# First weight block converted as two halves, with a new hand-written order on every engine

## The chip, the core and the metric

The kernel runs on one core of one Trainium2 chip. The core has a matrix engine (PE, with its weight loads shown as PEld), three elementwise engines (DVE, ACT, POOL) and a queue engine, SP, which issues all DMA transfers of this kernel. The metric is the device time of one execution in microseconds (us), from the chip's own clock; lower is better.

## The reference

The computation has two parts. The first is a linear attention with a decaying state, over 4 batches, 8 heads, 768 tokens and 48 values per head:

```python
def _attn_ref(r, k, v, w, u):
    state = np.zeros((B, H, D, D), dtype=np.float32)
    for t in range(S):
        kt, vt, rt = (k[:, :, t], v[:, :, t], r[:, :, t])
        cur = np.einsum('bhd,bhe->bhde', u[None] * kt, vt)
        y[:, :, t] = np.einsum('bhd,bhde->bhe', rt, state + cur)
        state = w[None, :, :, None] * state + np.einsum('bhd,bhe->bhde', kt, vt)
```

Its output, reshaped to 3072 tokens by 384 columns, goes through a feed-forward net (FFN) with 2048 inner columns:

```python
    h = x @ w_in
    sp = np.maximum(h, 0.0) + np.log1p(np.exp(-np.abs(h)))
    g = h * erf(sp)
    return (g @ w_out).astype(np.float32)
```

## The kernel before

**Attention.** The 768 tokens of each batch are cut into chunks of 128, which gives 24 chunks (6 per batch), numbered so that chunk g belongs to batch g mod 4. Each chunk is loaded by SP, its r and k are scaled (`prep_r`, `prep_k`), the matrix of token pairs is made on PE (`a_step`, tiles A), masked into `am` by DVE, and multiplied with the values on PE (`y_step`, tile y). `ds_product` makes what the chunk adds to the state `sbd`. Four chunks make one FFN input block of 512 tokens: ACT writes the high part of x from y (`x_hi`), DVE the low part (`x_lo`).

**FFN.** There are 6 blocks of 512 tokens and 16 slices of 128 inner columns, which gives 96 steps, numbered 0 to 95. Step n is `f1` (9 matmuls of 512 columns into a tile h, of which there are three), six ACT and two DVE operations on it (`act_a` to `act_h`; the last, `act_h`, casts to `gh`), a subtraction to `gl` (`act_l`, DVE or POOL), and `f2` (9 matmuls into three accumulators). The tiles s1, s2, gh and gl have two buffers each. Two matrices of the split-precision weights stand in SBUF, a high part and a low one (`wih`, `wil` for the input side, `woh`, `wol` for the output side).

**Weights.** The weights arrive as 64-bit floats in 8 blocks of 768 columns per matrix. `fetch_w` loads a block, `load_w` converts it in six parts: a (ACT), b, c and d (DVE), e (ACT, the high part) and f (DVE or POOL, the low part). The working tile wt has one buffer, so that one block is in conversion at a time. A block of the input side serves two FFN slices; the first block serves slices 0 and 1. The names C00a to C00f in the order stand for the six parts of the first input block.

**Order.** No scheduler decides the order. `ORDER` is a list of some 1,750 words that is read from left to right, and each word issues one operation; each engine works through its own operations in that order and waits where an operand is not there. A letter names the operation (f, a, b, z, c, d, e, g, h, l and p are those of an FFN step, in this order; A, P, Y, X, D, S, M, Q, N, K, R, E belong to attention; L and F are loads, C the conversions, O the output). The number is the chunk, the step or the block. A trailing + puts the operation on POOL, a * on ACT, neither on DVE; @ names PSUM banks. W with a number is that many dummy matmuls on a tile of zeros (`keep_warm`), of which there are 16 before the first word and 10 in the list. `late.close()` frees the staging tiles after the last C word.

**The end.** The last step is 95. Its three outputs are copied out of the accumulators by ACT (o95_0 and o95_2, the latter in two halves) and DVE (o95_1) and sent by SP. The word Z (`count_bad`) makes a count on PE and DVE that every engine reads with a TENSOR_LOAD, since a general path behind a branch handles decays outside a range.

Of the kernel before, what the change touches and what calls it, by code (L numbers as in the profile page):

```python
# [848 lines left out]
N3* C10a W2 L4b Q4a+ Q4b V2@h L5a W3 M20* L3b C10b Q4c T0 D3@2 C10c P20 Y2@h M40+ M41* C10d L5b Q5a C10e C10f+ K5+ N4
F01 R5+ Q5b Q5c X1b A4@h3 N2* S3a* S3b* Y3@0 X2a D2@h X3a X2b S2b* X3b f0 C01a P41 S2a C01b P40 L6a C01c R6 M51* L6b  # L850
Q6a+ M50* a0 K6 C01d b0 F02 z0 Y4@1 X4a A5@43 P51 C01e C01f+ f1 D4@0 c0 P50 d0 Q6b+ X4b S4b S4a e0 g0 L7a C02a C02b
Q6c C02c a1 b1 Y5@4 X5a X5b z1 f2 M60* c1 C02d C02e K7 M61+ A6@41 d1 N5 f3 P61 D5@2 P60 C02f+ S5b h0 a2 N6+ e1 S5a g1
F11 L7b C11a b2 C11b h1 l0 Y6@0 z2 a3 b3 D6@2 X6a S6b S6a c2 d2 l1+ e2 f4 C11c p0 p1 a4 Q7a C11d z3 C11e g2 h2 C11f
Q7b+ Q7c f5 l2+ c3 X6b F03 C03a C03b C03c p2 C03d R7 d3 e3 g3 M71* A7@01 C03e C03f f6 F12 a5 h3 l3+ b4 P71 b5 C12a z4
c4 z5 a6 C12b C12c M70+ P70 c5 d4 e4 C12d d5 g4 p3 C12e C12f e5 g5 L9a h4 l4+ Y7@1 X7a F13 X7b f7 b6 z6 h5 f8 a7 C13a
l5 C13b C13c b7 c6 d6 L9b Q9a+ e6 z7 c7 d7 C13d F05 C13e e7 K9 p4 g6 h6 p5 f9 a8 F14 g7 h7 l6 C13f+ p6 l7+ p7 b8 z8
L8a K8+ C05a C05b C05c a9 b9 z9 c8 d8 e8 C05d g8 c9 O70a O70b h8 f10 R9 f11 R8 C05e C05f d9 e9 g9 Q9b Q9c l8+ a10 O72a
O72b M91+ b10 z10 C14a h9 l9 O71a a11 b11 A9@01 S4c f12 p8 p9 c10 d10 z11 c11 e10 S4d+ C14b C14c d11 e11 g10 h10 C14d
M90 C14e l10 L8b C14f+ g11 a12 b12 z12 f13 a13 P90 h11 l11+ c12 Q8a+ Q8b+ F04 b13 z13 d12 e12 p10 g12 C04a C04b C04c
N9 c13 d13 f14 p11 f15 a14 C04d b14 h12 S5d l12 C04e C04f p12 F15 e13 g13 Q8c M80+ a15 b15 f16 z14 h13 l13+ P91 z15  # L860
c14 A8@01 d14 e14 p13 C15a c15 g14 d15 e15 C15b a16 h14 C15c f17 b16 C15d C15e S5c+ g15 O71b N7 l14 h15 f18 a17 M81+
b17 z16 c16 d16 e16 l15+ z17 P81 c17 C15f+ P80 p14 p15 F06 C06a O150a g16 h16 d17 a18 O152a C06b C06c e17 f19 C06d b18
a19 Y9@0 O150b l16 g17 h17 l17+ N8 O151a C06e z18 C06f b19 z19 D7@1 F07 p16 c18 C07a C07b F16 C07c d18 e18 c19 d19 g18
# [130 lines left out]
```

## Time and profile before

| | |
|---|---|
| time, median of 3 runs | 507.01 us (506.83 to 507.46) |
| profiled execution, own time | 506.34 us |
| its span, first to last instruction | 504.6 us |
| PE busy | 489.5 us, 97% of the span |
| PEld busy | 384.1 us, 76% |
| ACT busy | 401.4 us, 80% |
| DVE busy | 356.1 us, 71% |
| POOL busy | 200.8 us, 40% |
| chain that ended last, by engine | PE 93%, DVE 3%, ACT 2%, issue 1% |
| chain, by line | L540 (f1) 41%, L599 (f2) 40%, all attention products under 3% each |

The shares of busy time are averages over the whole span, while the limits differ by stage. A stage is therefore read by its own window. "Granted clock" (PEclk) is the share of TensorE's full clock that the chip gave it: 1.00 is 2.4 GHz, 0.50 is 1.2 GHz. An idle time is shown with what ended it.

### The profile page before, as it was taken

The numbers are of one execution on the slowest core, as the hardware profiler recorded it, in microseconds if no ns is written. First come the engines' busy times: TensorE is split into PE (matmuls) and PEld (weight loads), VectorE is DVE, ScalarE is ACT, GpSimd is POOL, SyncE is SP. The second block draws the span as 40 slices with busy tenths as digits, with TensorE's granted clock in tenths as the row PEclk, the third lists the DMA queues.
The fourth block names the chain that finished last, engine by engine and source line by source line (L and its number), as shares of the span: only waits on it lengthen the run. The fifth ranks groups of instructions, "written<-read, shape, count | busy, mean of one in ns | idle before, by whom it ended". The sixth has DMA issues, their size and how long they took to land.

```text
span 504.6 us, 11104 instructions
## 1 busy us (share of the span) xinstructions
PE 489.5 (97%) x4463; PEld 384.1 (76%) x4464; DVE 356.1 (71%) x574; ACT 401.4 (80%) x772; POOL 200.8 (40%) x185
## 2 busy tenths in 40 slices
PE   7799999999999999999999999999999999999993
PEld 3567877777877788777777887778777787878882
DVE  7999999989887777776888758475465675424531
ACT  4778999999988878868678687768886977888881
POOL 6656434352352665236867644103212521121010
PEclk9989999999999999999999999999999999999998
DMA  8647453522741423214522340500120010100001
GB/s 310 215 166 268 147 176 126 182 99 57 257 162 31 148 96 136 83 50 183 158 96 65 123 150 2 188 1 21 31 108 22 6 38 1 62 1 0 1 1 68
DMA packets 15737, 50.92 MB, mean 101 GB/s; under 512 B 1856, under 2 KB 2752, under 8 KB 15680
## 3 DMA queue, kind: packets, MB, share of 16 engines
q1 hardware_dynamic: 15680, 50.15, 29.2%
q8 instruction: 37, 0.61, 0.5%
q14 instruction: 20, 0.16, 0.1%
HBM read 43.85 MB, written 6.29 MB: 99 GB/s over the span
## 4 chain that ended last, share of the span: by engine, by line
PE 93%; DVE 3%; ACT 2%; issue 1%; POOL 0%; DMA 0%; DVEq 0%; ACTq 0%
PE h L540 41%; PE acc L599 40%; PE y L474 3%; PE y L326 2%; PE A L300 2%; PE A L442 2%; PE ds L493 1%; PE kt L389 0%; DVE att L350 0%; DVE am L448 0%; PE dummy L104 0%; POOL att L363 0%; DMA wu<-in_wcol_dram 0%; DVE att L354 0%; DVE pw L193 0%
## 5 line engine op out<-in xcount | busy, mean ns | idle before, releaser
L540 PE MATMUL h<-x,wih 128*128 128x512 f32 x576 | 184.0, 400 | 0.4 <-ACT sbd L505 0.4
L583 POOL TENSOR_TENSOR gl<-s,gh 128x512 fp32r<-128x512 f32 x46 | 61.9, 1346 | 178.6 <-ACT gh L578 159.6
L540 PEld LDWEIGHTS h<-x,wih 128*128 128x128 f32 x576 | 106.7, 188 | 27.8 <-ACT x L514 0.7
L599 PE MATMUL acc<-gh,woh 128*128 128x512 f32 x288 | 115.8, 402 | 0.0
L599 PE MATMUL acc<-gl,woh 128*128 128x512 f32 x288 | 114.5, 398 | 0.2 <-DVE gl L583 0.2
L599 PE MATMUL acc<-gh,wol 128*128 128x512 f32 x288 | 114.1, 396 | 0.0
L540 PE MATMUL h<-x,wil 128*128 128x512 f32 x288 | 114.1, 396 | 0.0
L572 DVE SCALAR_TENSOR_TENSOR s<-s,h 128x512 f32<-128x512 f32 x96 | 65.4, 684 | 60.2 <-ACT s L568 59.7
L556 DVE SCALAR_TENSOR_TENSOR s<-s,h 128x512 f32<-128x512 f32 x96 | 65.5, 684 | 37.9 <-ACT s L551 21.7
L560 ACT ACTIVATE s<-s 128x512 f32<-128x512 f32 x96 | 60.1, 627 | 21.2 <-DVE s L556 20.9
L547 ACT ACTIVATE s<-h 128x512 f32<-128x512 f32 x96 | 56.4, 589 | 24.9 <-PE h L540 24.6
L578 ACT CAST gh<-s 128x512 fp32r<-128x512 f32 x96 | 58.6, 614 | 20.8 <-PE acc L599 9.5
L599 PEld LDWEIGHTS acc<-gh,woh 128*128 128x128 f32 x288 | 54.2, 188 | 14.1 <-issue 0.4
L599 PEld LDWEIGHTS acc<-gl,woh 128*128 128x128 f32 x288 | 54.3, 188 | 13.6 <-DVE gl L583 1.1
L540 PEld LDWEIGHTS h<-x,wil 128*128 128x128 f32 x288 | 54.2, 188 | 13.1
L599 PEld LDWEIGHTS acc<-gh,wol 128*128 128x128 f32 x288 | 54.2, 188 | 13.0
L564 ACT ACTIVATE s<-s 128x512 f32<-128x512 f32 x96 | 60.0, 628 | 1.8
L568 ACT ACTIVATE s<-s 128x512 f32<-128x512 f32 x96 | 60.1, 628 | 1.5
L551 ACT ACTIVATE s<-s 128x512 f32<-128x512 f32 x96 | 60.2, 629 | 1.1
L583 DVE TENSOR_TENSOR gl<-s,gh 128x512 fp32r<-128x512 f32 x50 | 37.3, 748 | 14.1 <-ACT gh L578 13.6
L279 POOL TENSOR_TENSOR am<-att,wr 64x512 f32<-64x512 f32 (+1 forms) x13 | 18.1, 1389 | 7.8 <-PE y L326 7.3
L408 POOL TENSOR_TENSOR att<-att 128x384 f32<-128x384 f32 x12 | 14.5, 1209 | 14.7 <-DVE att L404 12.7
(164 smaller groups left out, 572.6 us busy)
## 6 DMA issues: line engine op xcount, KB each, us to landing
att<-in_late_att_dram SPq DMA_DIRECT2D x12, 640.0 KB, 5.2
att<-in_att_dram SPq DMA_DIRECT2D x12, 512.0 KB, 4.9
raw<-in_win_dram SPq DMA_DIRECT2D x8, 768.0 KB, 6.3
raw<-in_wout_dram SPq DMA_DIRECT2D x8, 768.0 KB, 5.3
att<-in_late_att_dram SPq DMA_DIRECT2D x12, 512.0 KB, 4.0
att<-in_att_dram SPq DMA_DIRECT2D x8, 608.0 KB, 5.5
out_dram<-o SPq DMA_DIRECT2D x17, 256.0 KB, 2.8
att<-in_late_att_dram SPq DMA_DIRECT2D x12, 256.0 KB, 2.9
```

The source lines that it names most:

```text
L279: eng.tensor_tensor(out=late_am(g, half)[r], in0=by_head(chunks[g][r, 0:512]), in1=wr[r].rearrange("p a (b c) -> p (a b) c", b=2), op=ALU. ...
L540: nc.tensor.matmul(out=h, lhsT=w[:, f, q, :], rhs=x[:, xi, q, :], start=k == 0, stop=k == 8)
L547: nc.scalar.activation(out=s1, in_=e["h"], func=AF.Tanh, bias=FB0, scale=FA0)
L551: nc.scalar.activation(out=s1, in_=s1, func=AF.Tanh, bias=FB1, scale=FA1)
L556: nc.vector.scalar_tensor_tensor(out=e["s"], in0=e["s1"], scalar=FG, in1=e["h"], op0=ALU.mult, op1=ALU.add)
L560: nc.scalar.activation(out=s, in_=s, func=AF.Tanh, bias=FB2, scale=FA2)
L564: nc.scalar.activation(out=s, in_=s, func=AF.Square, bias=FB3, scale=FA3)
L568: nc.scalar.activation(out=s, in_=s, func=AF.Square, bias=FB4, scale=FA4)
L572: nc.vector.scalar_tensor_tensor(out=s, in0=s, scalar=FC, in1=ff[n]["h"], op0=ALU.subtract, op1=ALU.mult, reverse0=True)
L578: nc.scalar.copy(out=e["gh"], in_=e["s"])
L583: eng.tensor_tensor(out=e["gl"], in0=e["s"], in1=e["gh"].bitcast(F32), op=ALU.subtract)
L599: nc.tensor.matmul(out=acc[e], lhsT=w[:, f, es], rhs=g, start=first and i == 0, stop=last and i == 2)
```

## The change

The first 768 input columns are no longer converted in one pass of six parts. `load_w` makes two passes of 384 columns, C00a to C00f for the columns of slice 0 and C08a to C08f for those of slice 1; both read the same loaded block and both use the one working tile.

```diff
     def load_w(part, eng, which, g):
-        words = raws[which, g].bitcast(I32).rearrange("p (n two) -> p n two", two=2)
+        first = which == 0 and g in (0, NG)
+        c0, n = (g // NG * WG // 2, WG // 2) if first else (g * WG, WG)
+        raw, o = (raws[0, 0], c0) if first else (raws[which, g], 0)
+        words = raw[:, o:o + n].bitcast(I32).rearrange("p (n two) -> p n two", two=2)
         wl, wh = words[:, :, 0], words[:, :, 1]
         if part == "a":
-            bits[which, g] = stage.tile([P, WG], I32, tag="wt", name=f"wt{which}{g}", bufs=WTB)
+            bits[which, g] = stage.tile([P, WG], I32, tag="wt", name=f"wt{which}{g}", bufs=WTB)[:, 0:n]
...
-        s = slice(g * WG, (g + 1) * WG)
+        s = slice(c0, c0 + n)
...
-WG, RAWB, WTB = 768, 2, 1
+WG, NG, RAWB, WTB = 768, 8, 2, 1
...
 ORDER = """
-L0a K0 V0@0 L3a K3 W2 L1a R0 E0 K1 W3 R3 B0@1 J0* E3+ H0 Q0c* R1 A0@2h M00* P00 B3@1 J3* F00 H3 V1@h E1 L2a L0b L2b
+L0a K0 L3a L1a W2@2 L0b R0 E0 F00 B0@3 R3 J0* H0 K1 L2a C00a R1 E1 V0@h A0@10 V1@4 K3 C00b U0 Q0c* M00* P00 B1@h N0*
...
-b95 z95 h94 c95 d95 l94+ p93y p94z e95 p94x p94y g95 h95 l95 p95y O951a p95z O952a p95x O950a O951b O952b Z0 O950b
+l95 p95y p95z p95x O952a O950a O950b O951a O952b Z0 O951b
 """
```

The whole list is written anew: 1,762 words in place of 1,755. The operations are the same but for the six added parts and two dummy matmuls more (12 in the list in place of 10); their order, their PSUM banks and the choice between DVE, POOL and ACT differ on every engine. Line numbers after the diff's first hunk are 3 higher.

**Place 1, DVE ahead of FFN step 0.** wt00 and wt08 are the working tiles of the two conversions, raw00 the loaded block, am*c*_*h* the masked pairs of chunk c, x0 the input of block 0, which `f1` of step 0 reads. Before, a stretch with the conversion of all 768 columns:

```order
L137 TENSOR_SCALAR wt00_280<-wt00_280 128x768
L425 TENSOR_TENSOR am1_0_328<-ident_97,q1_320 128x512
L139 SCALAR_TENSOR_TENSOR wt00_280<-raw00_246,wt00_280 128x768
L354 TENSOR_TENSOR att2_255<-att2_255,wre_118 112x512
L448 COPY_PREDICATED am1_1_322<-mask_98,A1_1_303 128x512
L448 COPY_PREDICATED am1_0_328<-mask_98,A1_0_302 128x512
L142 SCALAR_TENSOR_TENSOR wt00_280<-raw00_246,wt00_280 128x768
L448 COPY_PREDICATED am3_1_386<-mask_98,A3_1_346 128x512
L375 COPY att2_255<-qp2_398 128x128
```

After, a stretch that ends at the low part of chunk 1 in x0:

```order
L520 TENSOR_TENSOR x0_356<-y0_281,x0_356 128x3x128
L378 COPY att2_205<-qp2_366 128x128
L140 TENSOR_SCALAR wt08_379<-wt08_379 128x384
L508 COPY sbd_160<-ds1_347 48x4x48
L142 SCALAR_TENSOR_TENSOR wt08_379<-raw00_194,wt08_379 128x384
L145 SCALAR_TENSOR_TENSOR wt08_379<-raw00_194,wt08_379 128x384
L357 TENSOR_TENSOR att4_321<-att4_321,wr_116 112x512
L353 TENSOR_TENSOR att4_321<-att4_321,wk_117 112x512
L520 TENSOR_TENSOR x0_356<-y1_392,x0_356 128x3x128
```

The three DVE parts of the second half (wt08) stand behind the low part of chunk 0 and ahead of that of chunk 1, so that they are ahead of step 0, whose `f1` reads all four chunks of x0.

ACT at the same place, up to its first operation of step 0 (s1_0 from h0). Before:

```order
L423 ACTIVATE am4_1_527<-ident_97,q4_475 128x128 x4
L145 CAST woh_91<-wt10_449 128x768
L396 COPY att2_255<-kt2_457 128x4x48 x2
L505 COPY sbd_160<-ds3_497 48x4x48 x2
L514 CAST x0_405<-y2_508 128x3x128
L514 CAST x0_405<-y3_568 128x3x128
L505 COPY sbd_160<-ds2_586 48x4x48
L135 ACTIVATE wt01_609<-raw01_539 128x768
L423 ACTIVATE am5_1_619<-ident_97,q5_543 128x128 x4
L423 ACTIVATE am5_0_626<-ident_97,q5_543 128x128 x4
L547 ACTIVATE s1_0_631<-h0_599 128x512
```

After:

```order
L426 ACTIVATE am2_0_529<-ident_97,q2_430 128x128 x4
L508 COPY sbd_160<-ds2_518 48x4x48
L426 ACTIVATE am4_0_575<-ident_97,q4_527 128x128 x4
L517 CAST x0_356<-y3_534 128x3x128
L148 CAST woh_91<-wt10_483 128x768
L517 CAST x0_356<-y2_553 128x3x128
L426 ACTIVATE am4_1_586<-ident_97,q4_527 128x128 x4
L138 ACTIVATE wt01_616<-raw01_509 128x768
L426 ACTIVATE am5_0_618<-ident_97,q5_614 128x128 x4
L550 ACTIVATE s1_0_637<-h0_625 128x512
```

Here 10 groups of four `am` activations stand ahead of step 0 in place of 8 on the whole engine; the added ones are for chunks 0, 1 and 4 (one each) while one of chunk 5 moved behind.

**Place 2, PE between steps 2 and 3.** A6 is the pair matrix of chunk 6, h3 the tile of step 3. Before:

```order
L442 MATMUL A6_0_785<-att6_615 64x128
L442 MATMUL A6_1_786<-att6_615 64x128
L540 MATMUL h3_805<-x0_405,wih_89 128x512 x2
L540 MATMUL h3_805<-x0_405,wil_90 128x512
L540 MATMUL h3_805<-x0_405,wih_89 128x512 x2
```

After:

```order
L445 MATMUL A6_0_776<-att6_580 64x128
L445 MATMUL A6_1_777<-att6_580 64x128
L104 LDWEIGHTS warm_86
L104 MATMUL dummy_804<-warm_86 128x512
...
L104 MATMUL dummy_804<-warm_86 128x512
L543 MATMUL h3_808<-x0_356,wih_89 128x512 x2
L543 MATMUL h3_808<-x0_356,wil_90 128x512
```

Three dummy matmuls now stand between A6 and step 3. The operand of A6 is scaled by `prep_r` of chunk 6, on DVE before and on POOL after. The tile of step 1 (h1) follows that of step 0 directly now.

**Place 3, the end on SP.** o95_1, o95_20, o95_21 and o95_0 are the outputs of step 95, fi the count. Before:

```order
L611 DMA out_dram<-o95_1_5614 128x512
L609 DMA out_dram<-o95_20_5619 128x256
L609 DMA out_dram<-o95_21_5620 128x256
L649 TENSOR_LOAD fi_180
L649 ISA x2
L611 DMA out_dram<-o95_0_5626 128x512
```

After:

```order
L614 DMA out_dram<-o95_0_5612 128x512
L612 DMA out_dram<-o95_20_5608 128x256
L612 DMA out_dram<-o95_21_5609 128x256
L652 TENSOR_LOAD fi_180
L652 ISA x2
L614 DMA out_dram<-o95_1_5615 128x512
```

The output that is sent first is o95_0 in place of o95_1, and o95_1 is the one behind the TENSOR_LOAD. On ACT and DVE the copies of the outputs stand as before.

## Rows read from the trace of the kernel before

**Rows 1.** Page, busy time and share of the span by engine, with instructions.

```profile
PE 489.5 (97%) x4463; PEld 384.1 (76%) x4464; DVE 356.1 (71%) x574; ACT 401.4 (80%) x772; POOL 200.8 (40%) x185
```

**Rows 2.** Windows: stretch in us, its length, busy time of each engine (x instructions), granted clock, DMA share, GB/s.

```profile
34.60:490.00 455.40, 455.36 (x3974) 361.69 (x3975) 323.74 (x504) 375.89 (x700) 178.54 (x154) 1.00 0.28 93
37.90:106.20 68.30, 68.30 (x618) 53.91 (x607) 63.82 (x97) 64.84 (x116) 31.35 (x23) 1.00 0.49 172
7.20:35.00 27.80, 22.88 (x449) 15.95 (x447) 25.23 (x41) 19.14 (x61) 17.02 (x14) 0.88 0.62 225
10.75:37.90 27.15, 23.09 (x469) 17.18 (x474) 24.64 (x40) 20.39 (x62) 16.50 (x11) 0.87 0.60 207
```

**Rows 3.** Windows of 2 us each in the start, the same columns.

```profile
20.00:22.00 2.00, 1.07 (x40) 0.80 (x31) 2.00 (x2) 0.60 (x2) 0.78 (x1) 1.00 0.90 342
24.00:26.00 2.00, 2.00 (x34) 1.67 (x34) 0.90 (x2) 2.00 (x7) 1.76 (x2) 0.50 0.98 301
```

**Rows 4.** Chain of waits in order of time: start, us, what.

```profile
24.05 1.92 PE A L442 x32
27.68 1.28 PE dummy L104 x3
34.64 2.51 PE h L540 x9
```

**Rows 5.** Timeline, ACT: start, us, instruction; then DVE.

```profile
10.77 0.27 ACT L375 COPY att<-qp 128x128 f32<-128x128 f32 x1 [1.92 <-DVE att L350]
16.18 1.28 ACT L423 ACTIVATE am<-ident,q 128x128 f32<-128x128 f32 x4
37.93 0.60 ACT L547 ACTIVATE s<-h 128x512 f32<-128x512 f32 x1
33.31 1.65 DVE L517 TENSOR_TENSOR x<-y,x 128x384 fp32r<-128x384 f32 x3
```

**Rows 6.** Groups of ACT, then POOL, by form: count, busy us, mean ns, idle before.

```profile
L145 ACT CAST wih<-wt 128x768 fp32r<-128x768 f32 x8 | 6.7, 837 | 3.1 <-DVE wt L142 3.1
L514 ACT CAST x<-y 128x384 fp32r<-128x384 f32 x24 | 11.1, 472 | 3.9 <-PE y L474 3.4 <-PE y L326 0.5
L354 POOL TENSOR_TENSOR att<-att,wr 112x512 f32<-112x512 f32 x2 | 3.1, 1548 | 0.0
```

**Rows 7.** Timeline, DVE and POOL side by side near 20 us.

```profile
19.50 2.10 DVE L142 SCALAR_TENSOR_TENSOR wt<-raw,wt 128x768 int32<-128x768 int32 x1
19.73 1.04 POOL L425 TENSOR_TENSOR am<-ident,q 128x512 f32<-128x512 f32 x1
```

**Rows 8.** Timeline, PE: dummy matmuls.

```profile
2.37 5.29 PE L104 MATMUL dummy<-warm 128*128 128x512 bf16 x16 [2.37 <-ACT warm L98]
27.48 1.49 PE L104 MATMUL dummy<-warm 128*128 128x512 bf16 x3
```

**Rows 9.** Timeline near 107 us: PE, then DVE, around step 12.

```profile
107.70 0.50 PE L599 MATMUL acc<-gl,woh 128*128 128x512 f32 x1
106.96 0.69 DVE L583 TENSOR_TENSOR gl<-s,gh 128x512 fp32r<-128x512 f32 x1
```

**Rows 10.** Timeline of the end: SP, ACT, DVE; then SP's longest own wait.

```profile
496.27 0.33 SPq L611 DMA_DIRECT2D out_dram<-o  x1
496.70 0.88 SPq L609 DMA_DIRECT2D out_dram<-o  x2
496.95 0.58 ACT L630 COPY o<-acc 128x512 f32<-128x512 f32 x1
497.08 0.15 DVE L648 TENSOR_REDUCE fi<-cnt 1x1 int32<-1x4 f32 x1 [0.76 <-PE cnt L647]
498.67 0.34 SPq L611 DMA_DIRECT2D out_dram<-o  x1
SPq L747 <- SPq L747: 2.7, 1, 2.7
```

More of the change, by code (lines that the diff above doesn't have):

```diff
@@ L849 @@
[L849 to L863, printed above, removed]
@@ new lines @@
+d10 l9 e10 z11 C14b g10 c11 C14c p8 d11 C14d F15 a12 p9 e11 g11 R8+ f13 h10 l10 C14e b12 a13 M91+ h11 C14f+ z12 f14
+l11 c12 b13 C04a z13 c13 C04b p10 d12 C04c e12 g12 N7+ O72b p11 f15 S5d+ d13 e13 K8+ C04d F06 h12 P91 g13 l12+ C04e
+C04f+ a14 O71b a15 P90 b14 h13 z14 l13+ b15 p12 C15a z15 C15b c14 d14 e14 f16 A8@01 c15 p13 d15 g14 e15 C15c h14 l14+
+C15d C15e g15 h15 f17 p14 a16 C15f l15 M81+ b16 a17 z16 b17 S6c+ N9+ C06a c16 z17 d16 P81 e16 p15 g16 c17 O150a F07
+f18 M80+ C06b C06c h16 P80 d17 l16+ e17 a18 g17 b18 C06d f19 h17 D7@3 D9@1 z18 O151a O150b O152a S7a a19 C06e l17+
@@ new lines @@
+Y9@0 S7b L10a p16 C06f c18 d18 L11a F16 S9a b19 z19 C07a C07b L11b O151b c19 C07c e18 d19 f20 g18 C07d e19 h18 C07e
+g19 p17 a20 C07f h19 l18 l19 b20 z20 O231a C16a C16b c20 f21 a21 S9b C16c f22 d20 p18 b21 F17 C16d z21 e20 p19 a22
+L10b g20 C16e c21 D8@1 Q10a+ C16f h20 S6d d21 b22 C17a K11 e21 l20 z22 c22 C17b f23 Q10b+ g21 d22 C17c e22 C17d a23
+p20 g22 h21 C17e b23 l21+ f24 h22 C17f f25 z23 S7d c23 l22 S7c+ d23 e23 g23 a24 a25 b24 p21 Q11a h23 O152b z24 l23
+O230a b25 c24 Q11b z25 Q11c d24 e24 X9a p22 R10+ c25 p23 S4c O231b X9b f26 d25 g24 Q10c h24 O231c e25 a26 g25 Y8@0 b26
@@ new lines @@
+R12a+ p30 S11b h31 l31 L14b L12c z32 S11a b33 R13a z33 O311a c32 d32 e32 c33 p31 d33 f34 e33 O311b S8c+ O312a a34
+O311c g32 h32 f35 g33 A12@01 h33 f36 b34 l32+ z34 M121* Q14a+ c34 d34 S9c+ a35 O310a O312b L13c e34 O310b l33+ G12a
+b35 a36 P120 p32 p33 g34 Q14b+ f37 Q14c z35 K14+ P121 h34 G12b+ S12a N13+ c35 b36 l34 d35 e35 g35 S10c+ z36 h35 c36
+d36 A13@01 G13a G13b+ a37 b37 l35+ S13a p34 f38 e36 P131 a38 P130 g36 O312c z37 c37 d37 Y13@0 h36 X13a Y12@1 M141 e37
+l36+ L15a L15b g37 M140 b38 f39 a39 b39 z38 p35 p36 c38 R14a f40 h37 R14b+ L16a d38 K15+ L16b e38 l37 S11c+ g38 z39
@@ new lines @@
+l51 c52 L22a a53 N19+ b53 d52 z53 e52 X17a g52 p50 f54 L22b p51 f55 R21b+ L19c a54 X17b c53 h52 A19@01 b54 d53 Q19c
+l52 z54 M191 M190+ e53 g53 p52 c54 d54 h53 l53 a55 R21a e54 b55 f56 Q21a z55 c55 d55 P190 L21c g54 a56 e55 b56 P191
+Q21b+ h54 f57 p53 l54 g55 z56 h55 c56 Q21c d56 e56 G19a a57 f58 p54 b57 l55+ G19b+ a58 z57 g56 p55 h56 f59 Y19@0 b58
+c57 d57 e57 g57 l56 h57 z58 O472b Q22a f60 a59 c58 d58 K21 p56 e58 b59 l57 S19a z59 L20a X19a c59 a60 S18c+ d59 g58
+e59 p57 b60 X19b g59 h58 h59 f61 l58 N21 z60 f62 M210+ a61 b61 l59+ c60 z61 d60 e60 a62 A21@10 R20a p58 c61 g60 Q22b+
@@ L911 @@
+g91 c92 p89 a93 d92 e92 h91 g92 O792b p90 l91 b93 z93 f94 h92 c93 d93 a94 l92 b94 e93 z94 g93 c94 p91 h93 O791b l93
+f95 d94 e94 a95 b95 g94 z95 p92 h94 c95 d95 p93y e95 l94+ p93x p93z p94y p94x g95 h95 p94z l95 p95y p95z p95x O952a
+O950a O950b O951a O952b Z0 O951b
 """
```

90 lines of the change are left out of this document (42 added, 48 removed).

## The prediction, made before the change was run

> **What bounds the kernel now.** I read the page's busy time first, then windows by stage, then the chain of waits. PE is busy for 489.5 us [rows 1], but that is an average of three stages. From the first FFN step to 490 us PE is busy 455.36 of 455.40 us at the full clock [rows 2]. There is nothing to win inside that stage except work taken off PE; every other engine has idle time there, but not everywhere: from 37.9 to 106.2 us ACT is busy 64.84 of 68.30 us and DVE 63.82 [rows 2], so that stage is nearly bound by three engines at once. Ahead of it lies the start, where PE waits for attention chunks to become x, and behind it the end. So the change can act in three ways: by the time at which step 0 can run, by new waits or new work on PE in the full stage, and by the end.
>
> The chain of waits through the start shows what sets step 0. PE idles near 21 us, its clock falls to 0.50 in the 2 us from 24.00 [rows 3], and the chain then runs through PE at half speed: the A products take 1.92 us and three dummies in that chain 1.28 us; step 0 starts at 34.64 [rows 4]. It starts before x is complete: DVE writes the low parts of the last three chunks in 1.65 us from 33.31 [rows 5], to 34.96, and the second matmul of step 0 reads them. That 34.96 is the number to compare.
>
> **The split itself.** The promise is that slice 1's half is converted behind the work for step 0. On DVE the order says otherwise: the three parts of the half wt08 stand ahead of the low part of chunk 1, and its two ACT parts ahead of the high parts of chunks 1 and 3. All six parts are still ahead of step 0. The split defers nothing past step 0, and it adds an instruction per part. A cast of 384 columns takes 472 ns against 837 ns for 768 [rows 6], so two cost 0.11 us more. No row shows the other parts at half size; I take the same 0.1 us for each of them, between 0 (exactly half) and 0.4 (a half costs three quarters of the whole). This is small, and it is counted inside the walk below.
>
> **When step 0 can run (-1.5 us).** What does change is the start's order. I walked the three engines by hand through the new order with durations of before, at the full PE clock. ACT takes the copy of the first q at 10.77 [rows 5] about 0.5 us earlier, since one scaling of another chunk is moved behind the product that it waits for. From there ACT has more to do until its first operation of step 0: ten groups of four `am` activations at 1.28 us [rows 5] instead of eight, 2.56 us, and 0.2 us for the halves, with small copies nearly in balance, so about 2.6 us more. Before, ACT is busy 20.39 of 27.15 us in that stretch [rows 2]. So it has 23.0 us of work from 10.3, and cannot reach step 0 before 33.3; with all of the old idle time it would reach it at 40.0. In the walk it has few waits, because the `am` groups no longer wait for POOL and PE: X high parts of chunks 0 and 1 near 19.0 and 22.8, the decay table `wkn` near 27.5, chunk 2's at 32.4, step 0's first activation near 36 instead of 37.93 [rows 5]. DVE waits once, near 27, for POOL's products on chunk 4, and finishes the last low part near 33.4. That is 1.5 us ahead of 34.96. Bounds: DVE is busy 25.23 of the 27.80 us from 7.20 [rows 2] and by count has the same work ahead of step 0 as before, so that it cannot finish before 32.4, 2.6 us ahead; on the other side 1.0 us behind, if PE's clock falls as before and ACT waits as before.
>
> What could help further is contention. The last DVE part of the first conversion took 2.10 us while a POOL operation of 1.04 us ran beside it [rows 7]; POOL has about 4 us less to do ahead of step 0 now. I count nothing for it, since the walk already uses the short duration; it is why the walk may hold. The Trainium skill, GPSIMD Engine Reference, section 1, Specifications, says that POOL's SBUF interfaces are shared with VectorE and contended by DVE instructions with two SBUF inputs; the stretched row has two such inputs, so the trace agrees there. By that rule alone the gain would be 1.1 us larger if before's sum had been walked with the short form; by the rows it stays at 1.5.
>
> **Dummies on PE (+0.6 us).** Three dummy matmuls now stand between A6 and step 3, in the full stage. Before, no dummy is there. Sixteen cost 5.29 us in a row, 0.33 each with the slow beginning; three at the half clock 1.49 us [rows 8]. At the full clock I take 0.2 us each, so 0.6 us, if PE has work waiting. The lower bound is 0, if PE waits at that place anyway; the upper is 1.5.
>
> **ACT and POOL behind step 0 (+0.9 us).** The walk gives more reasons to wait there. `prep_r` of chunk 6 moves from DVE to POOL, where the operation takes 1.55 us [rows 6], behind a conversion part that itself waits for ACT; A6 would wait for it up to 0.7 us, and the dummies and step 3 are queued behind A6 on PE. Then, up to the cast of step 12, ACT has about 2.3 us more (three groups of `am` come in, one goes out, some small operations move), while it had 3.46 us idle in the 68.30 us of this stretch [rows 2]. How near the edge that is can be seen at step 12: its `gl` is written in 0.69 us from 106.96, to 107.65, and PE takes it at 107.70 [rows 9]. There is no slack, and that `gl` goes to POOL in the new order. So of the start's gain, what the dummies leave is lost at the latest there: ACT begins its FFN work some 1.9 us earlier, has 2.3 us more to do, and POOL takes longer for the last link. I take 0.9 us, which makes PE even with before at step 12; bounds 0 (ACT uses its idle time) and 2.4 (it does not, and step 14 waits as well). Once lost, it stays lost, since PE is full from there to 490.
>
> **The rest of the full stage (0).** The FFN work and the attention groups are the same, the number of times that attention cuts into FFN work is the same within one. New orders of DVE, POOL and ACT are hidden as long as `gl` leads `f2`. Before, PE waits nowhere in this stage, so a new order can only equal that or lose: 0, with up to 1 us of loss.
>
> **The end (+1.3 us).** Here the order decides alone. Before, SP sends o95_1 at 496.27 and two halves from 496.70, for 0.88 us, then reads the count (ready at 497.23), and issues the last output at 498.67, 1.09 us after the halves; its data were ready at 497.53 [rows 10]. Now SP's first item is o95_0, the output that is ready last. The halves, ready long before, are queued behind it, and the TENSOR_LOAD and o95_1 behind them: issue of o95_0 near 497.6, halves to 498.9, the count's 1.09 us, last issue near 500.0. That is 1.3 us later, and the program ends after the last transfer (SP's wait of 2.7 us [rows 10]). ACT, DVE and PE finish at the same places, so nothing hides it. Bounds 0.9 and 1.7. In PE's last steps one `f2` fewer stands behind `f1` of step 95, which may give or cost half a microsecond; I count 0.
>
> **Sum.** -1.5 + 0.6 + 0.9 + 0 + 1.3 = +1.3 us. Against the profiled execution's 506.34 us this is 507.6; that execution was 0.7 us under the median of the three runs, 507.01, whose own range is 0.6 us. Against the median: **508.3 us**, 0.26% slower.
>
> **Rivals.**
> 1. *The start's gain is kept.* ACT uses its idle time, so the 0.9 falls away, or the dummies lie in a wait: -1.5 + 0.6 + 1.3 = +0.4, about 507.4, within 0.2%. For it speaks that DVE has some 2 us less to do up to step 12; against it the missing slack at step 12. Chance 0.30.
> 2. *Faster: the start runs without waits.* Before, the chain ran through PE at half speed; its two rows of 1.92 and 1.28 us [rows 4] would take half that at full speed, 1.6 us less, and DVE waited meanwhile (busy 0.90 of the 2 us from 24.00 [rows 3]). The new order spreads its dummies (1, 3 and 3 from about 23 to 27 us in the walk). If that keeps the clock up and DVE then works without a wait, the last low part is ready near its bound, 32.4; with the later dummies in a wait and no loss behind them this gives -2.6 + 1.3 = -1.3, so 505.7. It decides from a last low part before 32.7. Chance 0.14.
> 3. *The clock falls elsewhere, or ACT's debt is full.* In the walk PE idles 1.9 us near 8 to 10 us, because of the five dummies that stood there two are left, right behind the first sixteen; before, 0.93 us of idle time in the 2 us from 20.00 came ahead of the fall [rows 3]. A fall there would double the first A products and set the start back by up to 2 us: 510. The Trainium skill, TensorE: Matmul & The Clock Gate, section "What's actually happening", has the clock follow how busy PE has been lately, with the low level as the default; the trace agrees, as its fall follows an idle PE. By that rule the new gap is a danger and the price is that of this rival. Chance 0.14, with the full debt at step 14 (509.8) in it.
> 4. *The change does not do what it says.* That holds for the split in any case, as shown; if the reordered start gives nothing either, the sum is +0.6 to +1.3 plus 0.2, near 508.3, and no different from the forecast.
>
> **Chances and range.** The forecast, with rival 4, has 0.42. What can be told from no change here is about 0.2%, 1.0 us. The forecast's own spread, 507.4 to 509.4, puts a good part of it within that; with rivals 1 and 3: slower 0.48, same 0.37, faster 0.15. The range leaves out most of rival 2 and the worst of rival 3: 506.3 to 510.0.
>
> **What would show it.** The last output issue on SP about 1.4 us behind ACT's copy of o95_0 plus the halves' time, and a longer stretch from PE's last matmul to the end, by 1.3 us. DVE's last low part before step 0 near 33.4 and ACT's first activation of step 0 near 36. Three dummies ahead of step 3 without idle time before them. Waits of PE on `gl` or on A6 between 38 and 115 us, where before has none. The prediction is wrong if SP issues the last output no later, if the low part is ready before 32.7 and PE stays full, or if PE waits after 120 us.

## The result, and the profile after

The changed kernel takes 512.55 us (median of four executions, 511.33 to 513.64), the kernel before 507.24 beside it (506.83 to 507.93): a ratio of 1.011, interval 1.009 to 1.0129. It is slower, as forecast, but by 5.3 us where 1.3 were forecast, and outside the range of 506.3 to 510.0. The profiled execution took 511.33 us with a span of 509.3, against 506.34 and 504.6 before.

PE has as much to do as in [rows 1] and spends more of the span on nothing. From the page of the changed kernel, the busy times and then the chain that ended last:

```profile
PE 488.6 (96%) x4466; PEld 382.7 (75%) x4466; DVE 372.8 (73%) x582; ACT 397.7 (78%) x754; POOL 192.5 (38%) x179
...
PE 76%; DVE 13%; ACT 6%; issue 2%; DMA 1%; POOL 1%; SPq 0%; DVEq 0%; ACTq 0%; POOLq 0%
```

The share of PE in the chain fell from 93% to 76%, and DVE has 16.7 us more busy time though its instructions are nearly the same ones. Both point at DVE. The timeline of PE names the places; these are the idle times from step 0 on that it marks, and the three dummies (start, us, instruction, and in brackets the idle time before it and what ended it). The line at 47.27 is D5, the product that chunk 5 adds to the state:

```profile
31.60 0.49 PE L543 MATMUL h<-x,wih 128*128 128x512 f32 x1 [1.38 <-ACT x L517]
...
32.65 0.50 PE L543 MATMUL h<-x,wih 128*128 128x512 f32 x1 [0.56 <-DVE x L520]
...
43.73 0.82 PE L104 MATMUL dummy<-warm 128*128 128x512 bf16 x3
...
47.27 0.56 PE L496 MATMUL ds<-att 128*48 128x48 f32 x16 [0.62 <-DVE am L451]
...
79.30 0.73 PE L543 MATMUL h<-x,wih 128*128 128x512 f32 x2 [0.76 <-DVE s L575]
...
106.05 0.73 PE L543 MATMUL h<-x,wih 128*128 128x512 f32 x2 [0.17 <-DVE s L575]
...
275.75 0.33 PE L303 MATMUL A<-am,att 48*64 48x64 f32 x3 [0.68 <-DVE x L520]
...
284.57 0.50 PE L602 MATMUL acc<-gl,woh 128*128 128x512 f32 x1 [3.01 <-DVE gl L586]
...
499.12 0.51 PE L602 MATMUL acc<-gl,woh 128*128 128x512 f32 x1 [0.20 <-DVE gl L586]
```

In windows (stretch, length, busy time of PE, PEld, DVE, ACT and POOL, granted clock, DMA share, GB/s) the stage that answers to [rows 2] is full from 115 us on but for one piece:

```profile
37.00:47.00 10.00, 9.55 (x157) 6.90 (x153) 9.62 (x16) 9.38 (x23) 9.51 (x8) 1.00 0.59 203
47.00:57.00 10.00, 9.53 (x165) 7.92 (x166) 9.11 (x16) 9.91 (x20) 6.28 (x6) 1.00 0.55 187
115.00:255.00 140.00, 140.00 (x1376) 111.19 (x1378) 118.26 (x184) 110.87 (x202) 68.31 (x62) 1.00 0.36 121
255.00:290.00 35.00, 31.15 (x392) 24.15 (x380) 30.62 (x38) 21.57 (x38) 20.03 (x19) 1.00 0.30 99
290.00:490.00 200.00, 200.00 (x1498) 160.20 (x1497) 115.72 (x179) 156.35 (x281) 41.35 (x35) 1.00 0.12 42
```

Two of these stretches in the kernel before:

```profile
37.00:47.00 10.00, 10.00 (x195) 7.88 (x198) 9.79 (x16) 8.76 (x19) 6.54 (x5) 1.00 0.69 256
255.00:290.00 35.00, 35.00 (x563) 27.66 (x562) 29.36 (x41) 26.81 (x54) 25.31 (x22) 1.00 0.31 102
```

From 255 to 290 us PE is idle for 3.85 us; before, it was busy 35.00 of the same 35 us. In that stretch the biggest wait is 3.01 us, for `gl` of step 47. DVE, and below it POOL, at that place:

```profile
273.16 1.35 DVE L345 TENSOR_TENSOR att<-sbd,w 48x384 f32<-48x384 f32 x1
...
275.73 0.69 DVE L292 TENSOR_TENSOR am<-ident,q 64x512 f32<-64x512 f32 x1
...
278.41 4.91 DVE L292 TENSOR_TENSOR am<-ident,q 64x512 f32<-64x512 f32 x1
...
283.84 0.68 DVE L586 TENSOR_TENSOR gl<-s,gh 128x512 fp32r<-128x512 f32 x1
...
272.81 1.29 POOL L282 TENSOR_TENSOR am<-att,wr 48x512 f32<-48x512 f32 x1 [5.00 <-PE y L329]
...
277.52 1.29 POOL L282 TENSOR_TENSOR am<-att,wr 64x512 f32<-64x512 f32 x1
278.77 0.82 POOL L339 TENSOR_TENSOR att<-att,w 48x384 f32<-48x384 f32 x1
279.56 1.29 POOL L353 TENSOR_TENSOR att<-att,wk 112x512 f32<-112x512 f32 x1
280.82 1.00 POOL L361 TENSOR_TENSOR att<-att,wkn 128x384 f32<-128x384 f32 x1
281.78 0.98 POOL L407 TENSOR_TENSOR att<-att,ub 128x384 f32<-128x384 f32 x1
```

The same DVE instruction takes 0.69 us at 275.73. The next one begins at 278.41 and is held until POOL's five operations, which follow each other without a gap, have ended at 282.76; what is left after that is the 0.6 us of its own work. Behind it on DVE stands, after one operation of 0.67 us, the `gl` that step 47 needs. The wait of 0.68 us at 275.75, for a low part of x from DVE, looks the same: the DVE product at 273.16 takes 1.35 us where it takes 0.55 later (at 347.96), and ends 0.41 us behind POOL's operation of 272.81. A long DVE instruction is not a loss of PE's by itself: at 265.49 a `gl` took 2.87 us beside POOL and PE did not wait, and before, the longest stretched ones of this stretch took 1.77 to 1.86 us, with PE full.

The start, on the other hand, went better than forecast. The last low part of x0, on DVE, which answers to [rows 5], and two windows of the start, to [rows 3]:

```profile
32.05 0.55 DVE L520 TENSOR_TENSOR x<-y,x 128x384 fp32r<-128x384 f32 x1
```

```profile
24.00:26.00 2.00, 2.00 (x52) 1.48 (x51) 2.00 (x3) 1.36 (x4) 1.59 (x2) 1.00 0.78 260
34.00:36.00 2.00, 2.00 (x10) 1.62 (x9) 1.95 (x4) 1.97 (x7) 0.05 (x1) 1.00 0.78 318
```

It is ready at 32.60, 2.36 us ahead of the 34.96 before, and the clock stays at 1.00. The end on SP, which answers to [rows 10]:

```profile
501.92 0.33 SPq L614 DMA_DIRECT2D out_dram<-o  x1
502.30 0.93 SPq L612 DMA_DIRECT2D out_dram<-o  x2
504.26 0.33 SPq L614 DMA_DIRECT2D out_dram<-o  x1
```

The whole difference of the two profiled executions, 4.99 us, adds up like this. The first matmul of the last `f2` that reads `gl` comes at 499.12 in place of 494.78, 4.34 us later. Behind D5 at 47.27, PE waits for 0.20 (to 57 us) + 0.93 (at 79 and 106) + 3.85 (255 to 290) = 4.98 us; so at 47.3 it must still have been 0.64 us ahead (4.98 less 4.34). Of the 2.36 us of lead at step 0, 1.72 are gone by then. From 499.12 to the end of the span it takes 10.18 us against 9.82, 0.36 more; the time outside the span is 2.03 against 1.74, 0.29 more. 4.34 + 0.36 + 0.29 = 4.99.

### The profile page after: what moved, and what is told of

The parts are those of the page before. It is cut to its first block, busy times and chain, and to the rows that moved or that the text cites. A ratio compares the mean times of both kernels' runs of the same rounds, so it can differ in the third digit from the quotient of the medians.

```text
span 509.3 us, 11107 instructions
## 1 busy us (share of the span) xinstructions
PE 488.6 (96%) x4466; PEld 382.7 (75%) x4466; DVE 372.8 (73%) x582; ACT 397.7 (78%) x754; POOL 192.5 (38%) x179
## 4 chain that ended last, share of the span: by engine, by line
PE 76%; DVE 13%; ACT 6%; issue 2%; DMA 1%; POOL 1%; SPq 0%; DVEq 0%; ACTq 0%; POOLq 0%
PE h L543 35%; PE acc L602 34%; PE y L329 2%; PE y L477 2%; PE A L303 1%; DVE wt L142 1%; DVE wt L145 1%; DVE s L575 1%; DVE am L292 1%; DVE s L559 1%; ACT am L426 1%; DVE gl L586 1%; DMA att<-in_att_dram 1%; DVE wt L140 1%; ACT wt L138 1%
## 5 line engine op out<-in xcount | busy, mean ns | idle before, releaser
L586 POOL TENSOR_TENSOR gl<-s,gh 128x512 fp32r<-128x512 f32 x41 | 56.1, 1371 | 193.9 <-ACT gh L581 182.5
L586 DVE TENSOR_TENSOR gl<-s,gh 128x512 fp32r<-128x512 f32 x55 | 44.5, 812 | 19.9 <-ACT gh L581 19.7
L282 POOL TENSOR_TENSOR am<-att,wr 64x512 f32<-64x512 f32 (+1 forms) x12 | 15.9, 1327 | 22.7 <-PE y L329 22.5
L407 POOL TENSOR_TENSOR att<-att,ub 128x384 f32<-128x384 f32 x11 | 12.0, 1092 | 23.3 <-DMA att<-in_att_dram 21.1
```

Source lines behind the costliest of these rows:

```text
L282: eng.tensor_tensor(out=late_am(g, half)[r], in0=by_head(chunks[g][r, 0:512]), in1=wr[r].rearrange("p a (b c) -> p (a b) c", b=2), op=ALU. ...
L586: eng.tensor_tensor(out=e["gl"], in0=e["s"], in1=e["gh"].bitcast(F32), op=ALU.subtract)
```

## The experiments

A border is the moment at which one POOL operation ends and the next, right behind it, begins. **Theory.** DVE instructions whose operands lie in SBUF stand still while POOL works, for whole rows of POOL operations; the new order puts such a row beside the DVE work that feeds step 47. **Rival.** DVE and ACT are simply late since the start, and the waits would come without POOL. Times of before differ by a few tenths from one comparison to the next, so each kernel is set against the median of before that ran beside it. An order is changed by moving words; a word's letter, number and mark are those of the section on the kernel before.

**The split alone.** The order of before, with the second half's parts put in behind the first's.

```diff
-C00f+ Q2c M21* P30 V3@2 X0b
+C00f+ C08a Q2c C08b M21* C08c P30 C08d V3@2 C08e X0b C08f+
```

> The order of the kernel before, with only the split put in: the six parts of the first half stand where the six parts of the whole block stood, the six parts of the second half one by one behind them, all ahead of step 0. If the split itself costs about 0.1 us per part and hides beside other work, as predicted, the time is 507.0 to 507.8 us. If the split is what costs, because the second half sits on DVE and POOL in front of step 0, it is 509 us or more and step 0 starts later than 35.5 us.

510.89 us against 507.66 (ratio 1.0058, interval 1.0036 to 1.008). The parts' own price is small: on DVE 0.36, 0.56 and 0.54 us for the second half. But the working tile is now handed over twice. ACT waits 0.92 us for the second half's part d on DVE, and a copy that PE needs stands behind it: PE waits 2.10 us ahead of 28.38, the clock stands at 0.50 from 28 to 36 us, and the next conversion (wt10) begins at 29.3. Step 0 on PE:

```profile
39.18 1.09 PE L543 MATMUL h<-x,wih 128*128 128x512 f32 x2
```

Step 0 starts 4.5 us later. So the split is not neutral by itself in the old order; in the new order of the start x was ready earlier in spite of it. That the position chosen here for C08 is the best in the old order isn't claimed.

**The end of before.**

```diff
-p95y p95z p95x O952a O950a O950b O951a O952b Z0 O951b
+p95y O951a p95z O952a p95x O950a O951b O952b Z0 O950b
```

> The changed kernel with the last ten words in the order of the kernel before: o95_1 is sent first and o95_0 last, and step 95's three groups of products stand in the old order. The prediction gave this end 1.3 us; then the time falls by 1.0 to 1.5 us against the changed kernel. The first look at the trace of the changed kernel says otherwise: from the last matmul to the end of the span it takes 8.0 us, in the kernel before 7.7; by that the time falls by 0.3 us at most.

513.18 us, ratio 1.0094 (1.0067 to 1.0121), no faster than the changed kernel. The last issue on SP comes 3.88 us behind the last `f2`'s first matmul on `gl` in place of 5.14, as in before (3.89); so the 1.25 us on SP are real. But over all the profiles of this study the stretch from that matmul to the end of the span is 9.35 to 10.32 us with the old end (eight profiles, mean 9.89) and 10.18 to 10.53 with the new one (five, mean 10.33). The new end costs 0.4 us, not 1.3. The rest is made up behind SP's last issue: from there to the end of the span it takes 6.0 us in the mean with the old end (5.93 in the kernel before) and 5.2 with the new one (5.04 in the changed kernel). What shortens it was not found.

This profile also shows what the changed kernel's did not: the granted clock at 0.50 (1.2 GHz) behind PE's wait ahead of step 0, and again behind the one of 3.01 us. Two windows:

```profile
34.00:36.00 2.00, 2.00 (x7) 1.52 (x6) 1.92 (x4) 1.22 (x5) 0.06 (x1) 0.50 0.83 342
286.00:288.00 2.00, 2.00 (x5) 1.61 (x6) 1.94 (x4) 1.93 (x4) 0.00 (x0) 0.50 0.00 0
```

**POOL's row made shorter, DVE's work longer.**

```diff
-K17+ ... N17+
+K17 ... N17
```

> The changed kernel with two words of attention chunk 17 (prep_k, two operations, and the product with ub, one) on DVE in place of POOL. In the trace of the changed kernel they are the end of a row of five POOL operations without a gap, 277.5 to 282.8 us; a DVE multiplication of two SBUF operands begun at 278.41 lasts 4.91 us, to the end of that row, and PE then waits 3.0 us for gl of step 47. Theory (a DVE instruction with two SBUF operands stands still until POOL's row has a gap): the row is shorter by three operations, that DVE instruction is below 2 us, the wait at step 47 is below 0.7 us and the time falls by 2 to 3 us, although DVE gets about 2 us more work. Rival (DVE and ACT are simply behind there, and the long duration is a wait of another kind): more work on DVE makes the wait longer, 3.0 us or more, and the time is the same or up to 2 us longer.

510.55 us against 507.66 (1.0063, interval 1.0041 to 1.0085): 2.9 us above the kernel before, where the changed kernel was 5.3 above. The run above, which has the changed order but for the end, took 2.6 us longer. DVE, POOL's last operation of the row, and PE:

```profile
280.64 2.71 DVE L292 TENSOR_TENSOR am<-ident,q 64x512 f32<-64x512 f32 x1
...
281.80 1.00 POOL L407 TENSOR_TENSOR att<-att,ub 128x384 f32<-128x384 f32 x1
...
284.61 0.50 PE L602 MATMUL acc<-gl,woh 128*128 128x512 f32 x1 [0.82 <-DVE gl L586]
```

The row now ends at 282.80, the DVE instruction at 283.35, and the wait for step 47 is 0.82 us in place of 3.01, though DVE has more to do. The bounds that were expected, below 0.7 us for the wait and below 2 us for the instruction, were not quite reached: the row's last operation (L407) belongs to chunk 19, not 17, and moved up, so that the row is shorter by two operations, not three. The rival is out for this wait.

**Where in the list the loss lies.** Two kernels with the order of one up to f1 of step 40 (some 240 us) and of the other from there.

```diff
-<order of the changed kernel>
+<order of before up to f40, without C08> <what is left, in the changed order>
```

> The kernel before, without the split, up to f1 of step 40 (some 240 us), and from there all that is left in the order of the changed kernel. Theory (the largest loss lies in the new order of attention chunks 15 to 18 beside steps 42 to 48, whatever the start was): PE waits about 3 us for gl of a step near 47 and another 0.5 to 1 us for x near 276, and the time is 509.5 to 511.5 us. Rival (the waits come from engines that were late since the start): PE waits less than 1 us there and the time is 506.5 to 508.5 us.

512.11 us against 507.53 (1.0088, interval 1.006 to 1.0117). The wait is there with a start that has nothing new, and the clock is 0.55 from 286 to 288 us behind it. DVE and PE:

```profile
278.54 4.92 DVE L289 TENSOR_TENSOR am<-ident,q 64x512 f32<-64x512 f32 x1
...
284.72 0.80 PE L599 MATMUL acc<-gl,woh 128*128 128x512 f32 x1 [3.03 <-DVE gl L583]
```

The time is 0.6 us above what was expected: the seam of the two orders adds a wait of 0.89 us at 235.7.

And the other way round:

```diff
-<order of the changed kernel>
+<order of the changed kernel up to f40> <what is left, in the order of before>
```

> The changed kernel's order up to f1 of step 40 (some 240 us), and from there all that is left in the order of the kernel before, the end among it. Theory (the start, the dummies and the debt up to step 12 cancel; what makes the changed kernel slower lies behind step 40): the waits of 0.62 us at 47, 0.76 at 79 and 0.17 at 106 stay, those at 276 and 284 are gone, and the time is 507.2 to 508.5 us, within 0.2 per cent of the kernel before or little over. Rival (the order up to step 40 costs as much by itself, and the waits come in another place): 510 us or more.

509.55 us against 507.13 (1.0041, interval 1.0015 to 1.0068). The waits at 276 and 284 are gone, those at 48, 80 and 107 are there, as expected; the time is 1 us above the band, between theory and rival. Of the 5.3 us that the changed kernel loses, 2.9 go with the order from step 40 on; 2.4 stay with the order up to there. In them are a seam again (0.92 us at 234), and the clock: it stood at 0.50 from 34 to 36 us, behind the wait ahead of step 0, and D5 came at 48.57 in place of 47.27.

```profile
48.57 0.56 PE L496 MATMUL ds<-att 128*48 128x48 f32 x16 [0.45 <-DVE am L451]
```

Its ten executions go largely with the mean granted clock of each: 507.4 and 507.6 us at 0.997, 510.8 to 511.6 at 0.984 to 0.987, though one of 507.9 is at 0.992. The changed kernel's four do so too: 511.33 at 0.996, 513.64 at 0.989.

**The dummies.**

```diff
-N6+ e1 W3@2 f3
+N6+ e1 f3
```

> The changed kernel without the three dummy products ahead of step 3. The prediction gave them 0.6 us; then the time falls by 0.6 to 0.8 us. Rival: the product of the state D5 behind step 3 waits for DVE anyway (0.62 us in the trace of the changed kernel), so that the dummies' time goes into that wait, and the time falls by 0.2 us at most.

512.70 us (1.012, interval 1.0085 to 1.0156): nothing gained. D5, on PE:

```profile
47.28 0.56 PE L496 MATMUL ds<-att 128*48 128x48 f32 x16 [1.20 <-DVE am L451]
```

It begins at 47.28 with or without them; the dummies' time went into its wait for DVE. The rival of this run was right.

**The clock ahead of step 0.**

```diff
-X2b N4+ f0
+X2b N4+ W6@h f0
```

> The changed kernel with six dummy products on a free h bank right ahead of f1 of step 0, where PE waits 1.4 us for x. In the two profiles of the new order so far that fell at 0.50 (33 to 36 us) the fall follows that wait, and step 0 takes 1.7 us longer; the changed kernel's own profiled execution did not fall. Theory (the wait brings the clock down in a part of the executions, which is why the changed kernel's runs spread from 511.3 to 513.6): the clock stays at 1.00 from 30 to 40 us, the spread shrinks to the low end, and the median falls by 0.8 to 1.7 us. Rival (the spread comes from somewhere else): the median stays within 0.4 us, or rises by up to 1 us because the dummies delay step 0.

513.74 us (1.0131, interval 1.0106 to 1.0157). The clock stays at 1.00 from 30 to 40 us, but step 0's second matmul comes at 33.32, and in this profile the clock fell behind the wait at step 47 instead. The theory's gain did not come; on the spread the run decides nothing.

**Keeping the start's gain.** Four hybrids tried to keep the lead of 2.4 us and drop the rest.

```diff
-<order of the changed kernel>
+<order of the changed kernel up to f2> <what is left, in the order of before>
```

> The changed kernel's order up to f1 of step 2, and from there all that is left in the order of the kernel before. Theory (the new start is worth 2.0 to 2.3 us and the whole loss lies behind it, in the new order of the full stage): 505.0 to 506.0 us, faster than the kernel before, with PE's waits behind 60 us below 0.5 us in sum. Rival (the early start is lost at once, because ACT and DVE are in debt from 37 to 106 us): PE waits 1.5 us or more between 37 and 115 us and the time is 506.7 to 508 us.

506.89 us against 507.66 (0.9993, interval 0.9972 to 1.0014): the same as before. PE waits 0.57 us at 40.9 (the low part wil on POOL) and 1.66 at 46.1 (x on DVE), 2.2 in sum, and behind the second the clock stood at 0.50 from 48 to 50 us: nearly all of the lead is gone by 47 us, where the changed kernel had lost 1.7 of it. The next run was to take away both waits:

```diff
-K5 K6 C01c Q6a f1 C01d ... e1 W3@2 f3 <changed order>
+K5 C01c Q6a f1 C01d K6 ... e1 f3 <what is left, in the order of before>
```

> The changed kernel's order up to f1 of step 3, without the three dummies ahead of it and with prep_k of chunk 6 one conversion part later on DVE (it stood ahead of the parts whose last one, on POOL, f1 of step 2 waited 0.57 us for), and from there all that is left in the order of the kernel before. The hybrid that switched at step 2 lost 2.2 us of PE's time at 40.9 and 46.1 us and was equal to the kernel before. Theory (the new start is worth 2.0 to 2.3 us if PE does not wait between steps 2 and 4): PE waits below 0.8 us in sum from 37 to 60 us and the time is 505.3 to 506.5 us beside 507.3 for the kernel before. Rival (DVE is the bound there, so that each wait taken away returns one step later): PE waits 1.5 us or more up to 60 us and the time is 506.8 to 508 us.

508.62 us against 507.13 (1.0037, interval 1.0015 to 1.006). The wait at 40.9 is gone; 0.51 at 48, 1.20 at 52 and 0.74 at 65 came, and the clock fell at 33. The last two took away the wait ahead of step 0, one in the kernel that switches at step 40, the other in one that switches at step 6 and has no W3@2 ahead of f3:

```diff
-Q5b S3b* S2b* ... A4@03 R5 X3b F02 Q5c C01a M50* X2b N4+ f0
+S3b* S2b* ... A4@03 X3b X2b Q5b R5 F02 Q5c C01a M50* N4+ W4@h f0
```

> The order of the run before (the changed kernel's up to f1 of step 40, then that of the kernel before) with two edits ahead of step 0: DVE writes the last two low parts of x ahead of a sum of chunk 5 that waits for POOL (1.19 us in that run), and four dummy products on a free h bank fill PE's wait of 1.4 us. In that run's profile the clock fell to 0.50 from 33 to 36 us, right behind PE's waits of 1.39 and 0.85 us, its D5 came 1.3 us later than in the changed kernel's profile, where the clock did not fall, and its executions spread from 507.4 to 511.6. Theory (these waits bring the clock down in most executions, and that is the rest of the loss): the clock is 1.00 from 30 to 40 us, the low part is there by 32.2, the median falls by 1.0 to 2.0 us, to 507.4 to 508.5, and the spread is below 2.5 us. Rival (the clock has nothing to do with it, or falls in another place): the median stays at 509.0 us or more.

510.49 us against 507.18 (1.0086, interval 1.0057 to 1.0115). Step 0 runs through from 31.61, and then (PE, DVE, POOL):

```profile
37.74 1.10 PE L445 MATMUL A<-att 48*64 48x128 f32 x32 [0.80 <-DVE att L353]
41.41 0.74 PE L543 MATMUL h<-x,wih 128*128 128x512 f32 x2 [0.90 <-ACT wih L148]
43.32 0.80 PE L543 MATMUL h<-x,wil 128*128 128x512 f32 x1 [1.17 <-POOL wil L150]
32.06 1.43 DVE L411 TENSOR_TENSOR att<-att 128x384 f32<-128x384 f32 x1
31.25 1.82 POOL L150 TENSOR_TENSOR wol<-wt,woh 128x768 fp32r<-128x768 f32 x1 [2.70 <-ACT woh L148]
```

The two DVE operations that had stood ahead of x now stand beside POOL's conversion (the first takes 1.43 us, and 0.56 in the changed kernel) and delay everything behind them: 2.87 us of waits where 1.8 had been taken away (1.39 and 0.85 in the run that it was made from, 0.41 left), and the clock stood at 0.50 from 44 to 46 us instead of 34 to 36.

> The same two edits, without the three dummies ahead of step 3, and with the order of the kernel before already from step 6 on. If nothing but the order from step 6 on loses time (waits of 0.76 us at 79 and 0.17 at 106 us, the row of POOL operations near 280 us, the end) and the clock stays up, PE is some 0.6 us ahead of the kernel before at 47 us and keeps it: 506.0 to 507.0 us, the same as the kernel before or 0.2 per cent faster. Rival (a switch of orders brings its own waits, as at step 2 and step 3): 508 us or more.

508.99 us against 507.18 (1.0052, interval 1.0034 to 1.0071): the same three waits and 1.18 us at 50. Each time as much waiting or more came one to a few steps later, as the rival of the second hybrid said. From 37 to 47 us DVE is busy 9.62 of 10 us in the changed kernel. That alone does not make PE wait: before, it was 9.79 of the same 10 with PE full, but there x was ready 2.4 us later. DVE had hardly any time to spare for a lead; POOL, at 9.51 us in place of 6.54, had none either, and which of the two sets the limit was not separated. None of these four kernels beats the kernel before.

**The stall by itself.** Two small kernels: one DVE instruction of 128x512 (`form(k)`) beside n POOL products of the same size; h2 lies in PSUM, and the copy of it sets when DVE's instruction comes. The second kernel adds one to four copies of 128 columns behind that copy.

```python
for i in range(n):
    nc.gpsimd.tensor_tensor(out=po[i], in0=go if i == 0 else pa, in1=pb, op=ALU.mult)
nc.vector.tensor_copy(out=dd, in_=h2)
form(k)
```

> A small kernel that leaves the whole computation out and writes zeros. It has 20 places: five forms of one DVE instruction of 128x512 (a product of two SBUF operands, a product of an SBUF and a PSUM operand, a scaling of one SBUF operand, a copy out of PSUM, a maximum along a row of SBUF), each beside a row of 0, 1, 2 and 5 POOL products of about 1.3 us that begins about 1 us earlier. Theory (DVE stands still until POOL's row ends): the product of two SBUF operands lasts about 0.7 us beside none or one, 2 us beside two and 6 us beside five; the forms with PSUM keep their 0.5 to 0.7 us in every place. Rival (the two engines share a bandwidth and both slow down): it lasts about twice its time, 1.4 us, beside two and beside five alike, and POOL's products get longer.

All five forms kept their 0.4 to 0.7 us: the instruction happened to begin 0.1 us ahead of the border between two POOL products. What moved was POOL: its next four products took 5.37 us beside the product of two SBUF operands, 5.11 beside the scaling and 4.93 beside the forms with PSUM and the maximum, so POOL waits for DVE as well. This run does not decide between theory and rival.

> A small kernel that leaves the whole computation out and writes zeros, as the one before it. There DVE's instruction came within 0.2 us of the border between two POOL products and began without a wait; POOL's next product was stretched by 0.45 us instead. Now the DVE instruction comes 0.2, 0.4, 0.6 and 0.8 us later, into the middle of POOL's second product of five (three forms: two SBUF operands, an SBUF and a PSUM operand, scaling of one SBUF operand). Theory (DVE has to wait for the end of POOL's row, not of the running product only): with two SBUF operands it lasts 4 to 5 us in the places that come in the middle. Second theory (it waits for the end of the running product only): 0.7 to 1.7 us in all places, and POOL's next product is stretched. Rival (no lock): 0.7 us everywhere. With a PSUM operand 0.7 us everywhere by all three.

DVE with two SBUF operands, 0.2 and 0.6 us further into the row; then with a PSUM operand; then a scaling of one SBUF operand; then POOL's products beside the first and the third:

```profile
8.30 1.52 DVE L40 TENSOR_TENSOR do<-da,db 128x512 f32<-128x512 f32 x1
26.34 0.93 DVE L40 TENSOR_TENSOR do<-da,db 128x512 f32<-128x512 f32 x1
43.21 0.68 DVE L42 TENSOR_TENSOR do<-da,hh 128x512 f32<-128x512 f32 x1
76.31 1.31 DVE L44 TENSOR_SCALAR do<-da 128x512 f32<-128x512 f32 x1
8.01 5.38 POOL L56 TENSOR_TENSOR po<-pa,pb 128x512 f32<-128x512 f32 x4
42.97 4.93 POOL L56 TENSOR_TENSOR po<-pa,pb 128x512 f32<-128x512 f32 x4
```

The second theory held here: DVE waits for the end of the running product only, and gets in at the next border (the product takes 0.68 us in the first small kernel without POOL, the scaling 0.42). With a PSUM operand nobody waits. In the full kernels it is not always so: the instruction at 278.41 was passed by four borders, in every profile of that order. In the kernel before, a DVE product of 48x512 that began at 289.56, on the border to POOL's next operation, missed that one and got in at the following border (1.83 us in place of 0.7). What decides at a border was not found; it stays open.

## Why the prediction was wrong, point by point

- **The split itself** (0.1 us a part): two halves take 0.1 to 0.2 us more than a whole, but for the low part on POOL, 2.3 to 2.5 us for two in place of 1.84, more than the bound of 0.4. That it defers nothing past step 0 was right.
- **When step 0 can run** (-1.5, last low part at 33.4): it was ready at 32.60, so -2.36. Rival 2 named this point, 32.7, and the clock staying up; its first half came true. The walk had ACT too late: it reached step 0 at 35.09 in place of 36, with 2.24 us of waits in place of 2.7 and 22.5 us of work in place of 23.0.
- **Dummies** (+0.6): 0, the lower bound. They lie in a wait of PE for DVE that the prediction did not see.
- **ACT and POOL behind step 0** (+0.9, bounds 0 and 2.4): mis-sized, and for other reasons. Dummies and debt were to cost 1.5 us by step 12. They cost 2.85: 1.72 us were gone at 47.3 and 1.13 more by step 12. That PE was then only 0.5 us behind the kernel before, where the forecast had it even, is luck: the start had gained 0.86 us more than forecast. And PE waited neither for `prep_r` of chunk 6 on POOL nor for `gl` of step 12; it waited for `am` and s from DVE (0.62, 0.76, 0.17).
- **The rest of the full stage** (0, "with up to 1 us of loss"): this is the step that failed. It cost 3.85 us in the profiled execution, and in three of five profiles with its long wait the clock fell behind it. A wait of PE after 120 us was among the prediction's own signs of being wrong. The reasoning was that PE waits nowhere there before, so a new order "can only equal that or lose", and then the loss was bounded by a guess. [rows 7] had shown the mechanism: a DVE operation, 0.95 us otherwise, stretched to 2.10 beside POOL. The prediction used it once, as help for the start, and did not ask where the new order puts POOL operations in a row beside DVE work that feeds `f2`. The five words of the row (R17b+, G18b+, K17+, N17+, Q19a+) stand far apart in the list, the last behind f50; but nothing held POOL between them (it has no idle time there), so it ran ahead of the list, and reading the list side by side with DVE's does not show the row. The rule that the prediction took from the Trainium skill, GPSIMD Engine Reference, section 1, Specifications, speaks of DVE instructions with two SBUF inputs, and both of these are such; the trace agrees in both places (2.10 and 4.91 us).
- **The end** (+1.3, bounds 0.9 and 1.7): SP's last issue came 1.25 us later, as worked out, but the program ended only 0.4 later. The error is in the sentence that nothing hides it: what follows the last issue is not of one length (5.93 us before, 5.04 after; SP's own wait in it, 2.7 us before, is 3.3 in the run of the split alone and 2.4 in three waits after).
- **The clock** stood in a rival only, for the first 10 us. The idle time that rival 3 feared came (1.06 us of the 2 us from 8, where the walk had 1.9), and the clock stayed at 1.00 there. Where it fell, in runs with this order, was behind the new waits at 31 and 282 us, and not in every profile; the changed kernel's own has neither fall. That such falls make most of the 2.3 us between the changed kernel's executions fits their granted clocks; the runs that should remove a fall moved it, so it was not shown by an edit.

For the mechanism there is a sentence in the Trainium skill, SBUF — State Buffer, section "SBUF: two separate sides": the port pair of VectorE and GpSimd is an exclusive lock that the first comer holds for its instruction while the other blocks. The small kernels agree (1.52 us in place of 0.68, to the end of the running POOL product). The full kernels go beyond it: 4.91 us is a wait over four further POOL instructions.

## What to carry to other kernels

A full matrix engine says how much a new order can win, not how much it can lose: for the loss, look in the new order for places where the engine that feeds it runs beside a gapless row of POOL operations with its own operands in SBUF, and price them, at worst, by the length of the row. A lead won at the start is worth only what the next stage can take; here DVE was busy 96% of the 10 us from 37 (98% before), and of 2.36 us 1.72 were gone within 15 us. A later issue on a queue costs its full length only if what follows it is fixed.

## What the runs showed of the hardware

- A DVE scaling of a single SBUF operand (fp32, 0.42 us) waits for POOL as well: 1.31 us. A DVE product with an operand in PSUM does not (0.68).
- POOL is held up in turn: four products take 5.38 us beside a DVE product of two SBUF operands, 5.11 beside a scaling, 4.93 beside a product with PSUM (0.45 and 0.18 us more).
- In the full kernels a waiting DVE instruction was passed by up to four borders between POOL operations (4.91 us); in the small ones by none (1.52 us at most). What decides is open.
- Five profiles have the 3-us wait at step 47 and differ in what follows it: the clock was 0.50 to 0.55 from 286 to 288 us in three (the end of before, the dummies ahead of step 0, the new order from step 40) and 1.00 in two (the changed kernel, and without the three dummies).
